# Fourth layer, first phase: two of four pairs of inner tiles by seven products of halves

## The chip, the cores and the metric

The kernel runs on one core of a Trainium2 chip. The metric is device time in microseconds (us) of one execution, as the median of several runs. Engines are called by short names: PE is TensorE, PEld its weight loads, DVE VectorE, ACT ScalarE, POOL GpSimd, and SP is the engine whose queue issues the loads and stores.

## The reference

Attention over 2 x 12 heads with scores capped by a tanh, then two feed-forward blocks on the 896 tokens that come out (2 batches of 448, 768 columns):

```python
scores = cap * np.tanh(scale * q @ k.T / cap)
x = softmax(scores) @ v                    # as (896, 768)
h = x @ w_in;   x = maximum(h, 0) ** 2 @ w_out       # w_in 768 x 2048, w_out 2048 x 768
h = x @ w2_in;  return h / (1 + exp(-h)) @ w2_out    # same shapes
```

## The kernel before, in words

**Layers and tiles.** After the attention there are four layers: a (times `w_in`, relu squared), b (`w_out`), c (`w2_in`, silu) and d (`w2_out`). The inner dimension of 2048 is cut into 16 inner tiles of 128, the tokens into two halves b of S = 448, the 768 outputs into six blocks of 128 rows m (two halves n of three). Every f32 operand is held as two f16 parts, high and low, and a product of blocks is three matmuls of 128x128 by 128x448 (`products`, L902): high by high, and each high by the other's low. The rounding part `high` is made by `act` (L844) or `dve` (L858), the rest by `low_part` (L202).

**Phases.** The layers alternate: a0 b0 a1 b1 a2 b2 c0 d0 c1 d1. Each phase of a or c makes a group of inner tiles, the phase of b or d behind it uses them at once. The plan "f" (L175) has phases of 4, 6 and 6 inner tiles in a and b, and 8 and 8 in c and d.

**Pairs.** `Pair` (L914) makes two inner tiles by two halves of tokens from halves of operands: seven products of halves, p1 to p7, each nine matmuls, in the place of eight. Three accumulator banks are reused, so ACT copies a bank away (k1 behind p1, k2 behind p6) before the product that overwrites it. For layer d as a consumer, the same scheme needs forms of the activations (`forms_of_blocks`, L1086: four subtractions and four splits for each pair) and of the weights (`pair_steps`, L392: four sums of halves and splits of 768, 768, 768 and 384 columns, in place of two of 768).

**Layer d.** Its first phase (d0) goes through `out_units` (L1124): 12 outputs (six row blocks by two halves), each 4 pairs of inner tiles deep, 24 matmuls in a bank. `end2` (L1235) copies a bank to a tile y2 with ACT, and SP sends it to DRAM, tensor `spill` (L1248). The second phase (d1, L1256 to L1350) does its four pairs by seven, in two groups of two pairs (`GROUP`); it brings y back from `spill` with 12 loads on SP into the tile that held the forms of x1 (L1257 to L1259), so they wait for the last product of c1, and DVE adds a bank to y in `sum_of` (L1262):

```python
            y3 = x1.rows()
            for n, b in ((1, 1), (0, 1), (0, 0), (1, 0)):
                for m in range(MN * n, MN * n + MN):
                    nc.sync.dma_start(half(y3[:, m], b), spill[m, :, b * S : b * S + S])
```

**What sets the order of the rest.** Weights arrive bent as integers, and are turned (ACT `head` L340, DVE `shift` L348), split into high and low f16 parts (L364) and kept in slots: 14 tiles of 768 columns (`hl`), taken as a ring (`slot` L286), and small ones for the rests. `Plan` (L121) says when each is used; `Stream.chunk` (L505) lays background steps of ACT and DVE between products by planned costs and due times. A step with an alternative (`either`, L193) changes engine if its own is further behind than `SLACK` (0.3). Tiles of intermediate results are a ring of seven (`rtile`, L881). `Forms` (L1352) does the same as a pair's forms for the input of c, called x1.

Of the kernel before, what the change touches and what calls it, by code (L numbers as in the profile page):

```python
# [26 lines left out]
def softcap_attention_relu2_silu(  # L27
# [90 lines left out]
    GROUP = 2  # L118
    PLAIN = (("a", 0), ("a", 2))

    class Plan:  # L121
# [3 lines left out]
        def __init__(self, *sizes, seven=()):  # L125
            self.seven = seven
            self.items, self.where, self.layer, self.use, self.starts = [], {}, [], {}, []
            self.t, self.most, self.phases = 0.0, max(sum(sizes, ())), {}
# [4 lines left out]
            self.paired = {self.where[w, f] for w in "ac" for f in range(0, FT, 2) if (w, f) not in PLAIN}  # L133
            self.paired |= {self.where[w, 0, f // KD] for w, ph in seven for f in range(*self.phases[w][ph], KD)}

        def add(self, w_i, w_o, a, b):
            t, use, where, items = self.t, self.use, self.where, self.items
            self.starts.append(t)
            for f0, f1 in self.phases[a]:
# [13 lines left out]
                if (b, self.phases[a].index((f0, f1))) in self.seven:  # L153
                    stage = KT // 2 * GROUP * UNIT / 4
                    for e in range(e0, e1):
                        for n in range(DM // NW):
                            i = where[b, n, e] = len(items)
                            items.append((tile_of(w_o, n * (FT // KD) + e), f"w{b}{n}_{e}"))
                            self.layer.append(b)
                        at = t + (e - e0) % GROUP * UNIT / 4  # L160
                        use[i - 1], use[i - 1, "s"] = at, at + 2 * stage
                        use[i], use[i - 1, "r"] = at + 4 * stage, at + 5 * stage
                        if (e - e0) % GROUP == GROUP - 1:
                            t += 7 * stage
# [95 lines left out]
    class Stream:  # L260


        def __init__(self, plan, tag, wpool, dt, watch):
# [1322 lines left out]
```

## Time and profile before

| what | us |
|---|---|
| median of 3 runs (503.84 to 504.8) | 503.94 |
| the profiled execution | 504.16 |
| its span in the trace | 502.3 |
| busy: PE, DVE, ACT | 492.3, 392.1, 340.9 |
| stage starts: a0, b0, a1, b1 | 87.1, 114.3, 141.6, 177.3 |
| a2, b2, c0 | 218.2, 254.3, 295.2 |
| d0, c1, d1, last PE work | 343.9, 398.4, 446.1, 496.4 |

The profiled execution's own time is 1.86 us longer than the span of its instructions. The stage starts are the first matmul of each stage on PE's timeline. The names of tiles in the rows carry the stage: `ac8f` is a bank of layer c at inner tile 8, `yd_0f` an output bank of d0, `p_4df` a bank of d1's first group (pairs 4 and 5), `yformsf` the forms of activations, `yf` the tile of y.

### The profile page before, as it was taken

How to read it: one execution, taken by the hardware profiler on the slowest of the kernel's cores; microseconds unless marked ns; L12 is line 12 of the kernel's file. 1: busy time of each engine (PE TensorE's matmuls, PEld its weight loads, DVE VectorE, ACT ScalarE, POOL GpSimd, SP SyncE). 2: the span in 40 equal slices, each digit the busy share in tenths (PEclk: the TensorE clock that was granted, in tenths of full speed). 3: DMA queues.
4: the chain of work that ended last, by engine and by line, in shares of the span. 5: the costliest groups of instructions: out<-in, count | busy, mean ns of one | idle time of the engine just before them, and what ended most of it. 6: DMA issues, size and time to landing. Idle time of an engine off the chain costs nothing.

```text
span 502.3 us, 7110 instructions
## 1 busy us (share of the span) xinstructions
PE 492.3 (98%) x2608; PEld 237.9 (47%) x2608; DVE 392.1 (78%) x770; ACT 340.9 (68%) x524; POOL 31.6 (6%) x33
## 2 busy tenths in 40 slices
PE   8999999999999999999999999999999999998995
PEld 4233233555555555554555554555555555554552
DVE  0778999999978898967888988889143469987863
ACT  5999995978779984568985668987242487670200
POOL 1002555300000000000000000000000000000000
PEclk9999999999999999999999999999999999999999
DMA  7746562234544554773341215643517122033014
GB/s 253 264 140 168 175 190 66 90 112 162 178 147 165 190 189 133 244 253 125 125 128 62 64 63 190 217 161 130 191 42 243 61 88 98 0 103 117 2 74 153
DMA packets 22387, 69.76 MB, mean 139 GB/s; under 512 B 2887, under 2 KB 14151, under 8 KB 22343
## 3 DMA queue, kind: packets, MB, share of 16 engines
q1 hardware_dynamic: 22308, 69.22, 41.5%
q8 instruction: 22, 0.36, 0.3%
q14 instruction: 23, 0.18, 0.1%
q0 software_dynamic: 32, 0.00, 0.0%
q10 hardware_dynamic: 2, 0.00, 0.0%
HBM read 63.64 MB, written 5.54 MB: 138 GB/s over the span
## 4 chain that ended last, share of the span: by engine, by line
PE 93%; ACT 2%; DMA 1%; DVE 1%; issue 1%; SPq 0%; DVEq 0%
PE px L633 7%; PE p_6df L906 4%; PE yb_5f L906 4%; PE yb_3f L906 4%; PE yb_1f L906 4%; PE yb_0f L906 4%; PE yb_4f L906 4%; PE yb_2f L906 4%; PE s_B L614 3%; PE s_A L614 3%; PE ha_0f L906 3%; PE ha_1f L906 3%; PE p_4df L906 2%; PE yd_3f L906 2%; PE yd_5f L906 2%; PE yd_4f L906 2%
## 5 line engine op out<-in xcount | busy, mean ns | idle before, releaser
L622 ACT ACTIVATE e_A<-s_A 128x896 f32<-128x896 f32 x18 | 15.9, 918 | 4.5 <-PE s_A L614 4.2
L622 ACT ACTIVATE e_B<-s_B 128x896 f32<-128x896 f32 x18 | 15.9, 917 | 3.9 <-PE s_B L614 3.6
L718 ACT ACTIVATE e_A<-e_A 128x896 f32<-128x896 f32 x18 | 16.5, 955 | 0.0
L718 ACT ACTIVATE e_B<-e_B 128x896 f32<-128x896 f32 x18 | 16.5, 953 | 0.0
L1265 DVE SCALAR_TENSOR_TENSOR yf<-p_6df,yf 128x448 f32<-128x448 f32 x15 | 9.2, 623 | 6.1 <-PE p_6df L906 6.1
L207 DVE SCALAR_TENSOR_TENSOR hl_64f<-u_64f,hl_64f 128x768 f16<-128x768 f32 x1 | 1.0, 957 | 15.9 <-ACT hl_64f L373 15.9
L653 DVE TENSOR_TENSOR total<-total,e_C 64x896 f32<-64x896 f32 x11 | 12.9, 1172 | 0.4
L207 DVE SCALAR_TENSOR_TENSOR hl_68f<-u_69f,hl_68f 128x768 f16<-128x768 f32 x1 | 1.0, 959 | 13.1 <-ACT hl_68f L373 13.1
L1265 DVE SCALAR_TENSOR_TENSOR yf<-p_4df,yf 128x448 f32<-128x448 f32 x15 | 9.0, 614 | 0.0
L207 DVE SCALAR_TENSOR_TENSOR x1f<-yaf,x1f 128x448 f16<-128x448 f32 x12 | 7.3, 619 | 1.7 <-ACT x1f L845 1.7
L649 DVE TENSOR_TENSOR total<-total,e_A 128x896 f32<-128x896 f32 x6 | 8.2, 1359 | 0.3
L845 ACT ACTIVATE x1f<-yaf 128x448 f16<-128x448 f32 x12 | 6.7, 571 | 2.3 <-DVE yaf L856 2.2
L647 DVE TENSOR_TENSOR total<-e_A,e_A 128x896 f32<-128x896 f32 x6 | 6.6, 1102 | 1.2 <-ACT e_A L718 1.2
L373 ACT ACTIVATE hl_80f<-u_81f 128x768 f16<-128x768 f32 x1 | 0.8, 843 | 9.9 <-DVE u_81f L398 9.9
L856 DVE TENSOR_TENSOR yaf<-yaf 128x448 f32<-128x448 f32 x12 | 7.4, 620 | 0.1
L845 ACT ACTIVATE ycf<-yd_4f 128x448 f32<-128x448 f32 x2 | 1.1, 544 | 8.0 <-PE yd_4f L906 8.0
L647 DVE TENSOR_TENSOR total<-e_B,e_B 128x896 f32<-128x896 f32 x5 | 6.5, 1294 | 0.0
L706 DVE RECIPROCAL r<-r 128x448 f32<-128x448 f32 x2 | 5.9, 2954 | 0.1
L236 ACT ACTIVATE junk<-x0f 128x896 bf16<-128x896 f16 x6 | 5.7, 947 | 0.3
L906 PE MATMUL p_4df<-yformsf,hl_72f 128*128 128x448 f16 x18 | 4.4, 352 | 1.5 <-DVE yf L1265 1.5
L649 DVE TENSOR_TENSOR total<-total,e_B 128x896 f32<-128x896 f32 x5 | 5.5, 1091 | 0.4
L731 DVE TENSOR_SCALAR gcap<-gcap 128x1 f32<-128x1 f32 x1 | 0.2, 155 | 7.2 <-ACT gcap L730 7.2
(1848 smaller groups left out, 1646.0 us busy)
## 6 DMA issues: line engine op xcount, KB each, us to landing
spill<-ycf SPq DMA_DIRECT2D x12, 224.0 KB, 1.9
yf<-spill SPq DMA_DIRECT2D x12, 224.0 KB, 5.3
out<-yf SPq DMA_DIRECT2D x12, 224.0 KB, 2.2
rb<-scratch SPq DMA_DIRECT2D x10, 224.0 KB, 3.9
raw_wb_0f<-in_moe_w_out SPq DMA_DIRECT2D x2, 768.0 KB, 5.7
raw_wb_1f<-in_moe_w_out SPq DMA_DIRECT2D x2, 768.0 KB, 4.3
raw_wb_2f<-in_moe_w_out SPq DMA_DIRECT2D x2, 768.0 KB, 4.3
raw_wb_3f<-in_moe_w_out SPq DMA_DIRECT2D x2, 768.0 KB, 4.3
```

Of the source, the lines that this page charges most:

```text
L207: nc.vector.scalar_tensor_tensor(lo, x, scale, hi, op0=ALU.mult, op1=ALU.subtract, accum_out=watch.low() if see else None)
L614: nc.tensor.matmul(sp[:, j, :S] if b is None else sp[head(b), j, :S], lhsT=qk[head(j), 1, 128 * c : min(128 * c + 128, S)], rhs=qk[head(j) ...
L622: nc.scalar.activation(t, sp[:, :, :S], AF.Tanh, scale=scale_s)
L633: nc.tensor.matmul(px[i][head(j), :S], lhsT=v_m[:, 3 * j + int(x[1])] if b is None else pr.vc[m][head(b), j], rhs=e[:, j] if b is None els ...
L647: nc.vector.tensor_tensor(t, ex[m, x[0] + "0"], e, op=ALU.add)
L649: nc.vector.tensor_tensor(total[i], total[i], e, op=ALU.add)
L653: nc.vector.tensor_tensor(t, t, ex[m, "C"][head(b)], op=ALU.add)
L718: nc.scalar.activation(ex[m, x], ex[m, x], AF.Exp, scale=scale_c)
L845: return Step("A", cols, lambda: nc.scalar.activation(at(out), at(src), func, scale=scale), list(deps))
L856: return Step(eng, cols, lambda: e.tensor_tensor(at(out), at(x), at(y), op=op), list(deps))
L906: nc.tensor.matmul(acc, lhsT=w(e_w, kk), rhs=x(e_x, kk), start=first and i == 0, stop=last and i == len(n) - 1, skip_group_check=more,)
L1265: return Step("D", S, lambda: nc.vector.scalar_tensor_tensor(yb, acc, to_y, yb, op0=ALU.mult, op1=ALU.add), list(deps))
```

## The change

In d0, pairs 0 and 1 (the first four inner tiles) go by seven products, and pairs 2 and 3 are accumulated plainly into the same banks: p2, p3 and p4 each carry a plain part for one of the outputs (0,0), (0,1) and (1,0), and a new bank "z" takes (1,1). `Plan` takes a table of groups for each phase. The results of d0 are now kept in tiles of the ring `rtile`, the first contribution by an ACT copy, later ones by DVE sums, and are spilled from there. `forms_tile` runs whatever steps of x1's forms are left before the forms of c's pairs are laid where they are. Slots for weights go to the one that is planned free first. `SLACK` is 1.0 for 0.3, `CAUTION` 0.5 for 0.6. Samples for the self-test of numbers are taken at other tiles.

```diff
--- before.py
+++ after.py
...
@@ -172,13 +176,13 @@
                     t += (e1 - e0) * KT // 2 * UNIT
             self.t = t

-    plans = {"f": Plan((4, 6, 6), (8, 8), seven=(("d", 1),)), "g": Plan((4, 4, 4, 4), (4, 4, 4, 4))}
+    plans = {"f": Plan((4, 6, 6), (8, 8), seven={("d", 0): (((0, 1),), (2, 3)), ("d", 1): (((0, 1), (2, 3)), ())}), "g": Plan((4, 4, 4, 4), (4, 4, 4, 4))}

     ACT_FIX, ACT_COL = 0.11, 0.00082
     DVE_FIX, DVE_COL = 0.075, 0.00105
     POOL_FIX, POOL_COL = 0.1, 0.0036
     HOP = 0.21
-    SLACK, CAUTION = 0.3, 0.6
+    SLACK, CAUTION = 1.0, 0.5
     LOAD, NEXT_LOAD = 4.5, 3.1

     class Step:
...
@@ -285,17 +289,17 @@

         def slot(self, i):
             if i not in self.hl:
-                j = len(self.slots)
-                self.slots.append(i)
-                at = j % self.nslots
+                j = len(self.hl)
+                at = self.freest(self.slots, self.nslots)[1]
+                self.slots[at] = i
...

         def rest(self, i):
             if i not in self.hl:
-                at = len(self.rests) % self.nrests
-                self.rests.append(i)
+                at = self.freest(self.rests, self.nrests)[1]
+                self.rests[at] = i
...
@@ -306,14 +310,18 @@
                 self.u[i] = self.wpool.tile([128, WT], F32, tag="u", bufs=self.nwords, name=f"u_{len(self.u)}{self.tag}")
             return self.u[i]

+        def freest(self, held, n):
+
+            return min((-1.0 if at not in held else self.freed.get(held[at], 1e9), at) for at in range(n))
+
         def is_free(self, key):
             if key[1:] == ("r",) if isinstance(key, tuple) else False:
-                n = len(self.rests)
-                return -1.0 if n < self.nrests else self.freed.get(self.rests[n - self.nrests])
-            n = len(self.slots)
-            if next(k for k in self.order if k not in self.hl) != key:
+                t = self.freest(self.rests, self.nrests)[0]
+            elif next(k for k in self.order if k not in self.hl) != key:
                 return None
-            return -1.0 if n < self.nslots else self.freed.get(self.slots[n - self.nslots])
+            else:
+                t = self.freest(self.slots, self.nslots)[0]
+            return t if t < 1e9 else None

         def room(self):
...
@@ -921,7 +929,7 @@
                 self.i = i = ws.todo.where[w, f]
                 self.forms = self.forms_at(i)
                 self.open, self.seeded = False, True
-                self.four = watch and (NEXT[w], [f0 <= f < f1 for f0, f1 in phases[w]].index(True)) in ws.todo.seven
+                self.four = ws.todo.where.get((NEXT[w], 0, f // KD)) in ws.todo.paired
                 self.blocks = {}

             @staticmethod
...
@@ -1113,6 +1122,18 @@
                 split("p7", r12, [t3], 9.0)
                 split("p4", r21, [t4], 10.0)
                 ends[ended[id(r11)]] = t2
+
+        forms_of = {}
+
+        def forms_tile():
+            if f0 not in forms_of:
+                for st in x1.steps:
+                    if st.end is None:
+                        ws.run_first(st)
+                forms_of[f0] = ytile("forms").rearrange("p m s -> p (m s)").bitcast(F16).rearrange(
+                    "p (n e s) -> p n e s", e=2, s=S
+                )
+            return forms_of[f0]

         def run_pairs(w, fs, x, funcs):
             for f in fs[::2]:
...
@@ -1221,15 +1242,12 @@
         for ph in range(len(phases["c"])):
             f0, f1 = phases["c"][ph]
             fs = range(f0, f1)
-            seven = ("d", ph) in ws.todo.seven
+            seven, plain = ws.todo.seven.get(("d", ph), ((), ()))
+            final = ph == len(phases["c"]) - 1
...
-            if seven:
-                forms = ytile("forms").rearrange("p m s -> p (m s)").bitcast(F16).rearrange(
-                    "p (n e s) -> p n e s", e=2, s=S
-                )
             run_pairs("c", fs, x1, silu)
-            if ph == 0:
+            if ph == 0 and not seven:
                 y2 = ytile("c")

...
@@ -1253,18 +1269,27 @@
...

-            y3 = x1.rows()
-            for n, b in ((1, 1), (0, 1), (0, 0), (1, 0)):
-                for m in range(MN * n, MN * n + MN):
-                    nc.sync.dma_start(half(y3[:, m], b), spill[m, :, b * S : b * S + S])
-            accs, steps = {}, {}
+            if final:
+                y3 = x1.rows()
+                for n, b in ((1, 1), (0, 1), (0, 0), (1, 0)):
+                    for m in range(MN * n, MN * n + MN):
+                        nc.sync.dma_start(half(y3[:, m], b), spill[m, :, b * S : b * S + S])
+            accs, steps, rows = {}, {}, {}

             def sum_of(n, b, m, acc, deps=()):

-                yb = half(y3[:, MN * n + m], b)
-                return Step("D", S, lambda: nc.vector.scalar_tensor_tensor(
-                    yb, acc, to_y, yb, op0=ALU.mult, op1=ALU.add
-                ), list(deps))
+                if final or (n, b, m) in rows:
+                    yb = rows[n, b, m] if not final else half(y3[:, MN * n + m], b)
+                    st = Step("D", S, lambda: nc.vector.scalar_tensor_tensor(
+                        yb, acc, to_y, yb, op0=ALU.mult, op1=ALU.add
+                    ), list(deps))
+                else:
+                    yb, free = rtile(f"y{n}{b}{m}")
+                    rows[n, b, m] = yb
+                    st = act(AF.Copy, yb, acc, free, scale=to_y)
+                if not final:
+                    ends[ended[id(yb)]] = st
+                return st

             def new(name, pool):
                 if pool == "q":
@@ -1274,15 +1299,18 @@
             def operand(p, f, e):
                 if p in ("p1", "p2", "p5", "p3"):
                     return half(g[f + (p in ("p2", "p3"))][:, e], int(p in ("p5", "p3")))
-                return forms[:, 3 * ((f - f0) // 2) + ("p6", "p7", "p4").index(p), e]
+                return forms_tile()[:, 3 * ((f - f0) // 2) + ("p6", "p7", "p4").index(p), e]

             def stored(n, b, m):
+                if not final:
+                    nc.sync.dma_start(spill[MN * n + m, :, b * S : b * S + S], rows[n, b, m])
+                    return
                 m += MN * n
                 if es[-1] < f1 // KD - 1:
                     return
                 nc.sync.dma_start(out[m * 128 : m * 128 + 128, b * S : b * S + S], half(y3[:, m], b))

-            def ended(p, m):
+            def behind(p, m):

                 us = UNIT / 4
                 if p == "p1":
@@ -1301,22 +1329,51 @@
...
                     st = steps["k3", m] = sum_of(1, 1, m, accs["a", m], [steps["k5", m]])
                     ws.chunk(us, st)
-                    stored(1, 1, m)
+                    if not plain:
+                        stored(1, 1, m)
                 elif p == "p3":
                     ws.chunk(us, sum_of(0, 1, m, accs["b", m], [steps["k2", m]]))
                     stored(0, 1, m)
-                else:
+                elif p == "p4":
                     ws.chunk(us, sum_of(1, 0, m, accs["a", m]))
                     stored(1, 0, m)
+                else:
+                    ws.chunk(us, sum_of(1, 1, m, accs["z", m], [steps["k3", m]]))
+                    stored(1, 1, m)

             needs = {"p2": "k1", "p6": "k1", "p7": "k2", "p3": "k5", "p4": "k3"}
...
-            groups = [range(e, e + GROUP) for e in range(f0 // KD, f1 // KD, GROUP)]
-            for es, p in [(es, p) for es in groups for p in ("p1", "p2", "p5", "p6", "p7", "p3", "p4")]:
-                for m, e in [(m, e) for m in range(MN) for e in es]:
+            def plain_products(p, m, e):
+
+                (n, b), bk = {"p2": ((0, 0), "c"), "p3": ((0, 1), "b"), "p4": ((1, 0), "a"), "z": ((1, 1), "z")}[p]
+                if (bk, m) not in accs:
+                    accs[bk, m] = new(f"z{m}", "p")
+                key = ws.todo.where["d", n, e]
+                hl = ws.get(key)
+                for kk in range(KD):
+                    ws.need(done[KD * e + kk, b])
+                first, last = p == "z" and e == f0 // KD + plain[0], e == f0 // KD + plain[-1]
+                products(
+                    accs[bk, m], lambda ew, kk: hl[:, ew, kk * NW + m * 128 : kk * NW + m * 128 + 128],
+                    lambda ex, kk: half(g[KD * e + kk][:, ex], b), range(KD), first, last, p != "z",
+                )
+                if m == MN - 1 and p in ("p3", "z"):
+                    ws.used(key)
+                if last:
+                    ws.chunk(UNIT / 4)
+                    behind(p, m)
+                else:
+                    ws.chunk(UNIT / 2)
+
+            order = ("p1", "p2", "p5", "p6", "p7", "p3", "z", "p4") if plain else ("p1", "p2", "p5", "p6", "p7", "p3", "p4")
+            groups = [range(f0 // KD + es[0], f0 // KD + es[-1] + 1) for es in seven]
+            for es, p in [(es, p) for es in groups for p in order]:
+                for m, e in [(m, e) for m in range(MN) for e in es] if p != "z" else ():
                     f, i = KD * e, ws.todo.where["d", 0, e]
                     key, at = Pair.forms_at(i)[p]
                     hl = ws.get(key)
+                    if watch and (ph, p, m, e) == (0, "p1", 0, 0):
+                        watch_later(hl[:, 0, :S])
                     if p in of_block:
                         k, b = of_block[p]
                         ws.need(done[f + k, b])
@@ -1330,22 +1387,26 @@
                     fresh = p in ("p1", "p5")
                     products(
                         acc, lambda ew, kk: hl[:, ew, at + m * 128 : at + m * 128 + 128],
-                        lambda ex, kk: operand(p, f, ex), range(1), fresh and e == es[0], e == es[-1], not fresh,
+                        lambda ex, kk: operand(p, f, ex), range(1), fresh and e == es[0],
+                        e == es[-1] and not (plain and p in ("p2", "p3", "p4")), not fresh,
                     )
                     if m == MN - 1 and p in ("p2", "p6", "p3", "p4"):
                         ws.used(key)
-                    if e == es[-1]:
-                        ended(p, m)
+                    if e == es[-1] and not (plain and p in ("p2", "p3", "p4")):
+                        behind(p, m)
                     else:
                         ws.chunk(UNIT / 4)
...
+                if p in ("p2", "p3", "p4", "z"):
+                    for e, m in [(f0 // KD + e, m) for e in plain for m in range(MN)]:
+                        plain_products(p, m, e)
...
```

On each engine the order moves as follows. On PE, the program has 18 matmuls and 18 weight loads fewer, all of them in d0 (270 for 288). The first place is DVE at the start of d1, from the first sum with the reloaded y on (`c_4df` and `p_4df` are banks, `hl` and `hr` weights, `gc` activations, `u` turned weights). Before:

```order
L1265 SCALAR_TENSOR_TENSOR yf<-c_4df,yf 128x448
L207 SCALAR_TENSOR_TENSOR gc14f,lows<-c11c14f,gc14f 128x448
L1265 SCALAR_TENSOR_TENSOR yf<-c_4df,yf 128x448
L856 TENSOR_TENSOR s5c14f<-s5c14f,c11c14f 128x448
L1265 SCALAR_TENSOR_TENSOR yf<-c_4df,yf 128x448
L856 TENSOR_TENSOR c21c14f<-c21c14f,s5c14f 128x448
L1265 SCALAR_TENSOR_TENSOR yf<-p_4df,yf 128x448
L207 SCALAR_TENSOR_TENSOR hl_77f,lows<-u_78f,hl_77f 128x768
L1265 SCALAR_TENSOR_TENSOR yf<-p_4df,yf 128x448 x2
L207 SCALAR_TENSOR_TENSOR yformsf,lows<-s5c14f,yformsf 128x448
L1265 SCALAR_TENSOR_TENSOR yf<-p_4df,yf 128x448
```

and in the change:

```order
L211 SCALAR_TENSOR_TENSOR gc14f,lows<-c11c14f,gc14f 128x448
L1283 SCALAR_TENSOR_TENSOR yf<-c_4df,yf 128x448
L864 TENSOR_TENSOR s5c14f<-s5c14f,c11c14f 128x448
L1283 SCALAR_TENSOR_TENSOR yf<-c_4df,yf 128x448
L864 TENSOR_TENSOR c21c14f<-c21c14f,s5c14f 128x448
L1283 SCALAR_TENSOR_TENSOR yf<-c_4df,yf 128x448
L211 SCALAR_TENSOR_TENSOR yformsf,lows<-u2c14f,yformsf 128x448
L1283 SCALAR_TENSOR_TENSOR yf<-p_4df,yf 128x448
L211 SCALAR_TENSOR_TENSOR yformsf,lows<-s5c14f,yformsf 128x448
L1283 SCALAR_TENSOR_TENSOR yf<-p_4df,yf 128x448 x2
L211 SCALAR_TENSOR_TENSOR yformsf,lows<-c21c14f,yformsf 128x448
L1283 SCALAR_TENSOR_TENSOR yf<-p_4df,yf 128x448
```

Both pieces end with the same sum, the seventh. The low part of the wide weight `hl_77f` and that of `gc14f` no longer stand among the sums; two more low parts of `yformsf` do.

The second place is SP's queue during d0 and c1, which issues the loads of weights (`raw_w...`) and the spills. Before:

```order
L281 DMA raw_wc15f<-in_moe_w_in 128x6144
L281 DMA raw_wd_4f<-in_moe_w_out 128x6144 x2
L1248 DMA spill<-ycf 128x448 x7
L281 DMA raw_wd_5f<-in_moe_w_out 128x6144 x2
L1248 DMA spill<-ycf 128x448
L281 DMA raw_wd_6f<-in_moe_w_out 128x6144
L1248 DMA spill<-ycf 128x448 x4
```

and in the change:

```order
L1306 DMA spill<-y002f 128x448
L285 DMA raw_wd_4f<-in_moe_w_out 128x6144 x2
L285 DMA raw_wd_5f<-in_moe_w_out 128x6144
L1306 DMA spill<-y010f 128x448
L1306 DMA spill<-y011f 128x448
L1306 DMA spill<-y012f 128x448
L285 DMA raw_wd_5f<-in_moe_w_out 128x6144
L1306 DMA spill<-y110f 128x448
L1306 DMA spill<-y111f 128x448
```

The spills stand singly or in threes between the loads, each from a tile of its own.

The third place is ACT in a0 (`x0` is the input, `ha` banks and tiles of layer a, `ga` its outputs, `zeros` the head of a turned weight). Before:

```order
L373 ACTIVATE hl_3f<-u_3f 128x768
L236 ACTIVATE junk,squares<-x0f 128x896 x6
L845 ACTIVATE ha_0f<-ha_0f 128x448 x3
L845 ACTIVATE ga0f<-ha_0f 128x448
L845 ACTIVATE ha_1f<-ha_1f 128x448 x3
L845 ACTIVATE ga0f<-ha_1f 128x448
L845 ACTIVATE ha_1f<-ha_1f 128x448
L845 ACTIVATE ga1f<-ha_1f 128x448
```

and in the change:

```order
L381 ACTIVATE hl_3f<-u_3f 128x768
L240 ACTIVATE junk,squares<-x0f 128x896 x4
L853 ACTIVATE x0f<-x_c11f 128x448
L853 ACTIVATE x_f0f<-x_c0f 128x448
L240 ACTIVATE junk,squares<-x0f 128x896
L354 ACTIVATE zeros<-raw_wb_1f 128x768
L853 ACTIVATE ha_0f<-ha_0f 128x448 x3
L853 ACTIVATE ga0f<-ha_0f 128x448
L853 ACTIVATE ha_1f<-ha_1f 128x448
```

The two forms of x0 were DVE's work before, and the weight `raw_wb_1f` is turned earlier.

## Rows read from the trace of the kernel before

**Rows 1.** Page: span, and per engine busy us (share of the span) xinstructions.

```profile
span 502.3 us, 7110 instructions
...
PE 492.3 (98%) x2608; PEld 237.9 (47%) x2608; DVE 392.1 (78%) x770; ACT 340.9 (68%) x524; POOL 31.6 (6%) x33
```

**Rows 2.** Page, the chain that ended last, shares of the span by engine.

```profile
PE 93%; ACT 2%; DMA 1%; DVE 1%; issue 1%; SPq 0%; DVEq 0%
```

**Rows 3.** Busy time by stage: a0, c0, d0, c1 and d1 in that order.

```profile
core 0: us, PE busy (x) PEld busy (x) DVE busy (x) ACT busy (x) POOL busy (x), PEclk, DMA share, GB/s
87.10:114.30 27.20, 27.20 (x146) 14.08 (x145) 26.60 (x51) 22.26 (x39) 4.41 (x5) 1.00 0.33 113
...
295.20:343.90 48.70, 48.02 (x253) 24.63 (x252) 41.87 (x94) 42.10 (x71) 0.00 (x0) 1.00 0.51 172
343.90:398.40 54.50, 54.50 (x290) 28.18 (x288) 20.70 (x47) 20.10 (x30) 0.00 (x0) 1.00 0.35 125
398.40:446.10 47.70, 47.70 (x255) 24.66 (x252) 42.02 (x103) 36.17 (x61) 0.00 (x0) 1.00 0.17 55
446.10:496.40 50.30, 48.48 (x255) 24.66 (x253) 37.26 (x85) 9.11 (x16) 0.00 (x0) 1.00 0.29 100
```

**Rows 4.** Timeline (start us, us, engine): first matmul of d0, of c1.

```profile
343.95 0.35 PE L906 MATMUL yd_0f<-gc0f,hl_50f 128*128 128x448 f16 x1
...
398.43 0.92 PE L906 MATMUL ac8f<-x1f,hl_58f 128*128 128x448 f16 x4
```

**Rows 5.** Page, groups: line engine op out<-in xcount | busy, mean ns | idle.

```profile
L207 DVE SCALAR_TENSOR_TENSOR hl_64f<-u_64f,hl_64f 128x768 f16<-128x768 f32 x1 | 1.0, 957 | 15.9 <-ACT hl_64f L373 15.9
...
L207 DVE SCALAR_TENSOR_TENSOR x1f<-yaf,x1f 128x448 f16<-128x448 f32 x12 | 7.3, 619 | 1.7 <-ACT x1f L845 1.7
...
L845 ACT ACTIVATE x1f<-yaf 128x448 f16<-128x448 f32 x12 | 6.7, 571 | 2.3 <-DVE yaf L856 2.2
...
L1265 DVE SCALAR_TENSOR_TENSOR yf<-p_4df,yf 128x448 f32<-128x448 f32 x15 | 9.0, 614 | 0.0
...
L373 ACT ACTIVATE hl_80f<-u_81f 128x768 f16<-128x768 f32 x1 | 0.8, 843 | 9.9 <-DVE u_81f L398 9.9
...
L856 DVE TENSOR_TENSOR yaf<-yaf 128x448 f32<-128x448 f32 x12 | 7.4, 620 | 0.1
...
L845 ACT ACTIVATE ycf<-yd_4f 128x448 f32<-128x448 f32 x2 | 1.1, 544 | 8.0 <-PE yd_4f L906 8.0
```

**Rows 6.** Timeline of DVE at the start of d1.

```profile
449.51 0.38 DVE L850 TENSOR_SCALAR yformsf<-u2c14f 128x448 f16<-128x448 f32 x1
...
454.94 0.62 DVE L1265 SCALAR_TENSOR_TENSOR yf<-c_4df,yf 128x448 f32<-128x448 f32 x1 [4.38 <-DMA yf<-spill]
```

**Rows 7.** Timeline of PE at its longest waits.

```profile
303.57 0.35 PE L906 MATMUL ac0f<-x_c0f,hl_40f 128*128 128x448 f16 x1 [0.63 <-ACT u2c0f L845]
...
233.31 0.35 PE L906 MATMUL ba12f<-x_f4f,hl_27f 128*128 128x448 f16 x1
233.90 0.35 PE L906 MATMUL aa12f<-x_c3f,hl_27f 128*128 128x448 f16 x1 [0.24 <-ACT ca12f L845]
...
461.84 0.73 PE L906 MATMUL p_4df<-yformsf,hl_72f 128*128 128x448 f16 x3 [1.53 <-DVE yf L1265]
```

**Rows 8.** Waits of SP: waiting line <- releaser: us in all, times, longest.

```profile
SPq L1259 <- PE ac14f L906: 24.6, 1, 24.6
```

**Rows 9.** All waits of PE after the attention (87.1 us on).

```profile
PE p_4df L906 <- DVE yf L1265: 1.8, 2, 1.5
PE ac0f L906 <- ACT u2c0f L845: 0.6, 1, 0.6
PE aa12f L906 <- ACT ca12f L845: 0.2, 1, 0.2
```

**Rows 10.** Timeline of ACT, the copy that PE waits for at 233.90.

```profile
233.33 0.53 ACT L845 ACTIVATE ca12f<-aa12f 128x448 f32<-128x448 f32 x1
```

More of the change, by code (lines that the diff above doesn't have):

```diff
@@ L117, in softcap_attention_relu2_silu, with __init__ @@
     PROD, UNIT = 9 * COL2, 12 * COL2
-    GROUP = 2
     PLAIN = (("a", 0), ("a", 2))
     class Plan:
-        def __init__(self, *sizes, seven=()):
+        def __init__(self, *sizes, seven={}):
             self.seven = seven
             self.items, self.where, self.layer, self.use, self.starts = [], {}, [], {}, []
-            self.t, self.most, self.phases = 0.0, max(sum(sizes, ())), {}
+            self.t, self.most, self.phases, self.paired = 0.0, max(sum(sizes, ())), {}, set()
             for w_i, w_o, a, b, size in ((w_in, w_out, "a", "b", sizes[0]), (w2_in, w2_out, "c", "d", sizes[1])):
@@ L132, in __init__ @@
                 self.add(w_i, w_o, a, b)
-            self.paired = {self.where[w, f] for w in "ac" for f in range(0, FT, 2) if (w, f) not in PLAIN}
-            self.paired |= {self.where[w, 0, f // KD] for w, ph in seven for f in range(*self.phases[w][ph], KD)}
+            self.paired |= {self.where[w, f] for w in "ac" for f in range(0, FT, 2) if (w, f) not in PLAIN}
         def add(self, w_i, w_o, a, b):
@@ L152, in add @@
                 e0, e1 = f0 // KD, f1 // KD
-                if (b, self.phases[a].index((f0, f1))) in self.seven:
-                    stage = KT // 2 * GROUP * UNIT / 4
+                groups, plain = self.seven.get((b, self.phases[a].index((f0, f1))), ((), ()))
+                if groups:
                     for e in range(e0, e1):
                         for n in range(DM // NW):
-                            i = where[b, n, e] = len(items)
+                            where[b, n, e] = len(items)
                             items.append((tile_of(w_o, n * (FT // KD) + e), f"w{b}{n}_{e}"))
                             self.layer.append(b)
[L160 to L164, printed above, removed]
+                    for es in groups:
+                        stage, more = KT // 2 * len(es) * UNIT / 4, KT // 2 * len(plain) * UNIT / 2
+                        for k, e in enumerate(es):
+                            i, at = where[b, 0, e0 + e], t + k * UNIT / 4
+                            self.paired.add(i)
+                            use[i], use[i, "s"] = at, at + 2 * stage + more
+                            use[i + 1], use[i, "r"] = at + 4 * stage + more, at + 5 * stage + more
+                        for e in plain:
+                            use[where[b, 0, e0 + e]] = t + 2 * stage
+                            use[where[b, 1, e0 + e]] = t + 6 * stage + 2 * more
+                        t += 7 * stage + 4 * more
                     continue
@@ L269, in __init__ @@
             self.raw, self.hl, self.ready, self.freed = [], {}, {}, {}
-            self.turned, self.slots, self.rests, self.order, self.u = [], [], [], [], {}
+            self.turned, self.slots, self.rests, self.order, self.u = [], {}, {}, [], {}
             self.words, self.read = [], {}
@@ L991, in out @@
                 a, self.done[ff, bb] = parts(r, hi, lo, after, to_g[self.w], self.w == "c")
-                if watch and ff == 0:
+                if watch and self.f == 0 and (ff, bb) in ((0, 0), (1, 1) if self.four else (0, 1)):
                     watch_later(hi, a)
@@ L1246, in end2 @@
                 ws.chunk(us, st)
-                if ph == 0 and ws.todo.seven:
-                    nc.sync.dma_start(spill[m, :, b * S : b * S + S], yb)
                 if ph == len(phases["c"]) - 1:
@@ L1378, in __init__, with later @@
             self.dt, self.scale, self.seen = dt, scale, {}
-            self.cells, self.more = {}, {}
+            self.cells, self.more, self.steps = {}, {}, []
             self.ready, self.highs, self.given, self.plain_end = {}, {}, set(), None
+        def later(self, *steps):
+            self.steps += steps
+            self.ws.later(*steps)
         def rows(self):
@@ L1418, in look @@
             c.due = self.due["p4", 0] - 4.0 if key in (1, 2) else self.ws.now + 60.0
-            self.ws.later(c)
+            self.later(c)
         def late(self, *last):
@@ L1432, in late @@
                         s.due = self.due[self.OWN[i % 4], i // 4] - 2.0
-                    self.ws.later(*own)
+                    self.later(*own)
                     st = own[-1]
@@ L1450, in split @@
             self.ready[p, j] = b
-            self.ws.later(a, b)
+            self.later(a, b)
             return b
@@ L1465, in minus @@
                 t.due = self.due[p, j] - 2.0
-                self.ws.later(t)
+                self.later(t)
                 return t
```

7 lines of the change are left out of this document (4 added, 3 removed).

## The prediction

> **What bounds the kernel now.** I read the page's busy shares first: TensorE (PE) is busy for 492.3 of a span of 502.3 us, VectorE (DVE) for 392.1 and ScalarE (ACT) for 340.9 [rows 1]. The chain of work that ended last says the same of the end: 93% of it is PE [rows 2]. An average hides stages, so I cut the span at the first matmul of each stage [rows 3]. In a0, c0, d0 and c1 PE is busy for the whole stretch or all but 0.7 us. Only d1 loses more: 48.48 busy of 50.30. So a change is worth the PE time that it removes, less what the other engines then add as waits, and the second is judged from DVE and ACT in the same rows. They are near full in c0 (41.87 and 42.10 of 48.70) and half idle in d0 (20.70 and 20.10 of 54.50).
>
> All PE work has one price. Layer d's first phase runs from 343.95 to 398.43 without a gap [rows 4]: 54.48 us for 12 outputs of 24 matmuls, 288 in all, or 0.1892 us for each, start to start.
>
> **The change, part by part.**
>
> *Products.* Plain, two inner tiles against two halves of the columns and two halves of the tokens are eight block products; the pairs cost seven. Per phase d0: the seven take 7 x 3 blocks of rows x 2 pairs x 3 split products = 126 matmuls, the two plain pairs 4 x 3 x 2 x 2 x 3 = 144, together 270 for 288. No other stage's count changes. That is 18 x 0.1892 = **-3.40 us**. All of it lies on the path, as rows 4 has no gap in which it could hide.
>
> *Work added for the seven forms*, by engine. Forms of the activations: 2 pairs x 4 subtractions x 0.620 = 5.0 on DVE; seven low parts in place of four for each pair, so 6 x 0.619 = 3.7 on DVE and 6 high parts x 0.571 = 3.4 on ACT. Forms of the weights: per pair four half-width sums (0.62 is their upper bound, from a wider tile) and 1.5 more splits, at most two at 0.957 on DVE and two at 0.843 on ACT: at most 2 x (2.5 + 1.9) = 8.8 and 2 x 1.7 = 3.4. Ends: 9 sums on DVE, which read a bank as the low parts read a tile, x 0.619 = 5.6, and 15 copies on ACT for 12, + 3 x 0.544 = 1.6 [rows 5]. DVE gets about 23 us, ACT 8.4. The order puts most of this into d0, whose DVE had 34 us idle; c0, c1 and d0 keep each engine below PE when I add up their instructions by these durations (c0: DVE some 3 us more, 45 of 48). The two pairs done by seven are those whose activations come out of the first half of c0, and their p6 and p7 come 17 and 20 us into d0 (p1, p2 with its plain part and p5 stand ahead: 18 + 54 + 18 matmuls). I cost the added work at **nothing**; its cover is PE's unbroken row of products, and if that cover fails the price is rival B's.
>
> *Moves between DVE and ACT.* The new slack makes the planner leave work on ACT that it used to hand over: 27 high parts go from a DVE form of 0.38 us to an ACT form of 0.571 [rows 5, 6]. DVE is relieved of 10 us, ACT takes 15. In a0 ACT was busy for 22.26 of 27.20 [rows 3]; about 4 us more still fit. The Trainium skill, page "ScalarE: Activation LUTs", section "Rules for kernel authors", speaks against this move: multiplications are better on VectorE than on ScalarE. The trace agrees on the single instruction, 0.38 against 0.571. Obeyed, it says that 27 x 0.19 = 5.1 us of engine time are wasted; whether that is time of the kernel depends on ACT setting an end, which is rival C. My sum counts zero.
>
> *The start of d1.* PE waits 1.53 us for a sum of DVE, at 461.84 [rows 7]. DVE itself had waited 4.38 us for the reload of y from the spill [rows 6], which SP issues only when PE's last product of c1 is done [rows 8]. The reload, its queue position and its trigger do not change, so the DVE wait stays. From the first sum to the seventh, which PE wants, DVE does 7 sums, 2 subtractions and 3 low parts, before as after; but before one of the three was the wide one of a weight (0.957 for 0.619), and it now lies ahead of the DVE wait. That saves about 0.33; a weight's shift now stands between two later sums and may give back some 0.15. I take **-0.2**; the ends are 0 and -0.33.
>
> *Spills and queues.* The 12 spills of d0 now leave from short-lived tiles and stand among the weight loads on SP, five loads behind a spill that waits for a sum. A late sum delays a load, thence weights. By the order those five bring weights of d1 and of c's last pair, used a stage later; and all that PE waits for after the attention is two sums of DVE and two copies of ACT, no load and no weight [rows 9], so nothing is charged. Slots in any order remove some DVE and ACT waits for a slot; PE has none of these, nothing again.
>
> Sum: -3.40 - 0.2 = -3.6. The profiled execution took 504.16 us, 0.22 more than the median of 503.94. So 504.16 - 3.60 = 500.56 there, and **500.3 us** for the median. Its own range is 499.7 to 501.2: DVE's stall of d1 wholly unmoved, or one or two new ACT waits of 0.4 as in rows 7, above; a little more recovered, below.
>
> **The rivals.**
>
> *A. The small stalls go as well.* Freer DVE and slots could remove the 0.40 that PE loses between 233.31 and 233.90 (0.59 for a step of 0.19) behind an ACT copy and the larger part of d1's wait (1.53). Against: the copy stood in an ACT queue without a gap ahead of it [rows 7, 10], and ACT gets more work. For: slots no longer taken in a ring, so that conversions spread out. 500.3 - 0.4 - 0.5 = 499.4 us.
>
> *B. DVE comes late in c0.* DVE goes from 42 to 45 of 48.7 there, and the first forms now force all leftover form steps of x1 out at once. Then each of c0's four pairs loses between 0.2 and the 0.8 that PE loses at 303.57 today (a start-to-start step of 0.98 for 0.189) [rows 7]: 0.8 to 3.1, so 501.1 to 503.4, in the middle 502.3 us. For it: the narrowest DVE margin of the program. Against: the added forms are due only in d0, with 17 us in hand.
>
> *C. ACT becomes the bound; slower.* Every pair of layers a and c has two products (p6, p7) that wait for an ACT copy of a bank (k1, k2). One other product of nine matmuls, 1.70 us, lies between; the copy takes 0.544, so ACT may be 1.1 us late before PE feels it. The wait of 0.24 before 233.90 is this case already [rows 7, 10]. With ACT at some 365 us for 341, and long forms of 0.84 in front of the copies, being late at each costs 14 pairs x 2 x 0.2 = 5.6 us, more than the products give: 500.3 + 5.6 = 505.9 us. It decides from an ACT backlog of more than 1.1 us at most copies. Against: of 28 copies two are felt now, and ACT has 18% free or more outside c0, where it gains nothing. The rule of the Trainium skill above would come out here: its 5.1 us, if all of them lay on the path, give 505.4.
>
> That the change doesn't do what it says is no rival: the order of PE has the 18 matmuls fewer.
>
> **How the numbers follow.** Chances: forecast 0.63, A 0.13, B 0.17, C 0.07. The range of 8 in 10 reaches from A's end to the lower half of B: **499.2 to 502.4**; outside lie C, the dearer part of B and some surprise below. Two tenths of a per cent, 1.0 us, is about what a measurement can tell from no change: faster means below 502.9, slower above 505.0. Faster: forecast, A and most of B, 0.87; same: B's dear end and a weak C, 0.08; slower: the rest of C, 0.05.
>
> **What would show it.** Right: d0 at about 51.1 us (270 x 0.1892) with no gap; c0 and c1 within 0.3 us of 48.6 and 47.7; d1's stall on the sum between 1.2 and 1.6; DVE busy in d0 above 30. B shows as PE waits for DVE in c0 and a c0 over 49.5; C as PE waits for ACT copies, many of them, in a1, a2 and c; A as a d1 below 49.8. The prediction is wrong if d0 keeps 54 us or if one stage other than d0 changes by more than 0.7 us.

## The result

The changed kernel takes 507.82 us (median of 7 runs, 505.8 to 510.91); the kernel before took 503.84 beside it. The ratio is 1.0077, 95% interval 1.005 to 1.0104: slower by 0.8%, where 0.7% faster was forecast. The profiled execution took 507.26.

The page of the changed kernel, span and busy time by engine, which answer to [rows 1]:

```profile
span 505.5 us, 7155 instructions
...
PE 490.9 (97%) x2590; PEld 236.5 (47%) x2590; DVE 397.3 (79%) x769; ACT 367.0 (73%) x589; POOL 30.8 (6%) x33
```

PE has less to do, as forecast, and the span is 3.2 us longer all the same. The stretches c0, d0, c1 and d1 in the view by stage (columns as in [rows 3]: length, then busy us of PE, PEld, DVE, ACT, POOL, granted clock, DMA share, GB/s):

```profile
294.30:343.70 49.40, 48.03 (x255) 24.66 (x253) 43.06 (x105) 40.85 (x75) 0.00 (x0) 1.00 0.29 97
343.70:394.75 51.05, 51.05 (x271) 26.40 (x270) 34.09 (x68) 26.67 (x42) 0.00 (x0) 1.00 0.49 170
394.75:450.55 55.80, 50.40 (x254) 25.30 (x253) 44.22 (x108) 40.44 (x70) 0.00 (x0) 0.94 0.23 78
450.55:499.65 49.10, 48.45 (x255) 24.65 (x253) 34.55 (x78) 9.39 (x17) 0.00 (x0) 1.00 0.29 102
```

From first matmul to first matmul, before and after: c0 48.76 and 49.35, **d0 54.48 and 51.08**, **c1 47.67 and 55.78**, d1 50.28 and 49.08. The attention and the six stages of a and b together are 0.9 shorter: a2 took 35.75 for 36.15, and the wait for `ca12f` of [rows 9] is gone, while a0 began 0.47 earlier, which lies within the 0.7 by which that start differs between the profiled executions here. So d0 gave its 3.40 us to the hundredth, d1 gave 1.2, and c1, whose products the change does not touch, took 8.1. Next, all that PE waits for in the changed kernel, which answers to [rows 9]:

```profile
PE bc8f L914 <- ACT y100f L853: 3.6, 1, 3.6
PE ac8f L914 <- ACT cc8f L853: 1.8, 1, 1.8
PE ac0f L914 <- ACT u2c0f L853: 1.3, 1, 1.3
...
PE p_4df L914 <- DVE yf L1283: 0.6, 1, 0.6
```

The first two are new, stand at the start of c1, and are copies on ACT. The timeline of PE there:

```profile
394.76 1.87 PE L914 MATMUL ac8f<-x1f,hl_72f 128*128 128x448 f16 x9
400.21 0.35 PE L914 MATMUL bc8f<-x_f0f,hl_73f 128*128 128x448 f16 x1 [3.59 <-ACT y100f L853]
...
401.95 0.58 PE L914 MATMUL bc8f<-x_f4f,hl_73f 128*128 128x448 f16 x1
404.34 0.53 PE L914 MATMUL ac8f<-x_c3f,hl_73f 128*128 128x448 f16 x1 [1.81 <-ACT cc8f L853]
404.67 0.58 PE L914 MATMUL ac8f<-x_c7f,hl_73f 128*128 128x448 f16 x1
```

The first product of c1 runs, then PE stands 3.59 us, does nine matmuls, stands 1.81 more. From about 401.5 the steps are 0.37 instead of 0.19: the clock, in the same stretch by windows.

```profile
401.50:408.20 6.70, 4.89 (x15) 1.93 (x13) 1.04 (x3) 3.08 (x6) 0.00 (x0) 0.50 0.63 213
```

Granted 0.50 there, that is 1.2 GHz of 2.4. The clock had stayed at 1.00 through the first stop (396.5 to 400.2). Between the end of its first product, near 396.6, and 401.5 PE had done six or seven matmuls. Counted from the step lengths, the two waits cost 3.8 and 2.2 us and the half clock another 2.2.

ACT, whose copies PE wants, in the same stretch:

```profile
377.93 0.84 ACT L381 ACTIVATE hl_84f<-u_69f 128x768 f16<-128x768 f32 x1 [2.56 <-PE p_0df L914]
391.55 0.84 ACT L381 ACTIVATE hl_85f<-u_71f 128x768 f16<-128x768 f32 x1 [12.78 <-PE p_0df L914]
...
399.64 0.53 ACT L853 ACTIVATE y100f<-p_0df 128x448 f32<-128x448 f32 x1
401.97 1.06 ACT L354 ACTIVATE zeros<-raw_wd_6f 128x768 f16<-128x768 bf16 x1 [1.80 <-DMA raw_wd_6f<-in_moe_w_out]
402.90 0.52 ACT L853 ACTIVATE y101f<-p_0df 128x448 f32<-128x448 f32 x1
403.31 0.55 ACT L853 ACTIVATE y102f<-p_0df 128x448 f32<-128x448 f32 x1
403.73 0.56 ACT L853 ACTIVATE cc8f<-ac8f 128x448 f32<-128x448 f32 x1
```

Here is the cause in one row: ACT stands 12.78 us, from 378.77 to 391.55, at the high part of the weight `hl_85f`, waiting for a product of PE (`p_0df`, in that stretch p4 of d0). Behind it in ACT's queue are two more heads and four more splits, then the copy `y100f` that frees a bank for `bc8f`, a head that waits 1.80 for a load, and `cc8f` (k1) only after that.

What product is that? `hl_85f` is laid into the slot of `hl_69f`, the n=1 weight of the first plain pair. The view of the tile `hl_69f` names who waited for it, and PE's timeline shows its last reader, in p4, just ahead of the split's start at 391.55:

```profile
who waited for it (us, times):
  ACT hl_85f L381: 12.8, 1
```

```profile
391.16 0.35 PE L914 MATMUL p_0df<-gc5f,hl_69f 128*128 128x448 f16 x1
391.35 0.35 PE L914 MATMUL p_0df<-gc6f,hl_71f 128*128 128x448 f16 x1
```

In the changed code that slot is declared free here:

```diff
+                if m == MN - 1 and p in ("p3", "z"):
+                    ws.used(key)
```

The n=1 weights are read by z and by p4, and the order of d0 is p1, p2, p5, p6, p7, p3, z, p4: z is not the last reader. The semaphores still protect the data, so ACT waits for p4; but the planner, which lays ACT's queue and takes "the slot that is free first", has the slot free 10.2 us too early: PE turns to the next weight at 381.14 in z, and at 391.35 in p4.

### The profile page after: what moved, and what is told of

It is laid out like the page before. It is cut to its first block, busy times and chain, and to the rows that moved or that the text cites. A ratio compares the mean times of both kernels' runs of the same rounds, so it can differ in the third digit from the quotient of the medians.

```text
span 505.5 us, 7155 instructions
## 1 busy us (share of the span) xinstructions
PE 490.9 (97%) x2590; PEld 236.5 (47%) x2590; DVE 397.3 (79%) x769; ACT 367.0 (73%) x589; POOL 30.8 (6%) x33
## 4 chain that ended last, share of the span: by engine, by line
PE 93%; DMA 2%; ACT 2%; DVE 1%; issue 1%; SPq 0%; DVEq 0%; ACTq 0%
PE px L641 7%; PE p_0df L914 7%; PE p_6df L914 4%; PE yb_4f L914 4%; PE yb_0f L914 4%; PE yb_5f L914 4%; PE yb_3f L914 4%; PE yb_2f L914 4%; PE yb_1f L914 4%; PE s_B L622 3%; PE s_A L622 3%; PE ha_0f L914 3%; PE ha_1f L914 3%; PE p_4df L914 2%; PE c_0df L914 2%; PE ac8f L914 1%
## 5 line engine op out<-in xcount | busy, mean ns | idle before, releaser
L853 ACT ACTIVATE c_6df<-p_6df 128x448 f32<-128x448 f32 x3 | 1.6, 528 | 6.5 <-PE p_6df L914 6.5
L914 PEld LDWEIGHTS <-hl_73f 128*128 128x128 f16 x18 | 2.2, 125 | 8.6 <-issue 7.9
```

The source lines that it names most:

```text
L853: return Step("A", cols, lambda: nc.scalar.activation(at(out), at(src), func, scale=scale), list(deps))
L914: nc.tensor.matmul(acc, lhsT=w(e_w, kk), rhs=x(e_x, kk), start=first and i == 0, stop=last and i == len(n) - 1, skip_group_check=more,)
```

## The experiments

Three theories. **M**: the mark behind z. **L**: ACT has too much to do since SLACK is 1.0, and is late whatever the slots (the forecast's rival C). **E**: the ends of d0 fall on c1's first pair and wait for tiles that are still being spilled.

**The mark moved** (`mark_p4`).

```diff
-                if m == MN - 1 and p in ("p3", "z"):
+                if m == MN - 1 and p in ("p3", "p4"):
```

> The changed kernel, with the two weights of the plain tiles of outputs n=1 declared free behind p4 instead of behind z, the product that comes before p4. Theory M (mark): ACT stood 12.78 us at the split hl_85f because its slot was declared free behind z while p4 still read it; the late copies y100f and cc8f then stopped PE in c1. Expected 507.8 - 8.2 (c1 took 55.8 us for 47.6) = 499.6 us, c1 within 0.3 of 47.7, no halved clock. Theory L (load): ACT is late at the end of d0 because SLACK 1.0 leaves it too much work, wherever a slot is marked: stays at 505 to 508. Theory E (ends): the copies of d0's last three outputs fall on c1's first pair and wait for tiles whose spill is under way: stays above 503.

Measured: 499.64 us (499.25 to 499.99) against 503.3 of before, ratio 0.9929 (0.9912 to 0.9945). Windows of c1 and d1, and ACT's timeline at the end of d0:

```profile
395.04:442.70 47.66, 47.66 (x253) 24.66 (x252) 38.39 (x96) 36.09 (x64) 0.00 (x0) 1.00 0.18 63
442.70:492.20 49.50, 48.47 (x255) 24.66 (x253) 34.68 (x79) 9.39 (x17) 0.00 (x0) 1.00 0.29 100
```

```profile
387.86 0.84 ACT L381 ACTIVATE hl_86f<-u_71f 128x768 f16<-128x768 f32 x1 [4.61 <-PE p_0df L914]
...
391.83 0.84 ACT L381 ACTIVATE hl_88f<-u_72f 128x768 f16<-128x768 f32 x1 [1.43 <-PE p_0df L914]
392.97 0.54 ACT L853 ACTIVATE y100f<-p_0df 128x448 f32<-128x448 f32 x1 [0.29 <-PE p_0df L914]
...
396.94 0.53 ACT L853 ACTIVATE cc8f<-ac8f 128x448 f32<-128x448 f32 x1 [0.43 <-PE ac8f L914]
```

c1 is back at 47.66 with no wait and a full clock. The weight that was `hl_85f` is now `hl_86f` and takes a slot that the p4 of the pairs gives up; ACT waits 4.61 us for it, to 387.86, and the copy `cc8f` starts 1.9 us after c1's first matmul, where it had started 9.0 us after. Theory M holds. That its number is met to 0.04 us is in part chance: the kernel before was 0.54 faster in this round than beside the result, and against it the step is 7.6, not 8.2 us.

**The order turned instead** (`z_last`): the mark stays behind z, and z becomes the last product.

```diff
-            order = ("p1", "p2", "p5", "p6", "p7", "p3", "z", "p4") if plain else ("p1", "p2", "p5", "p6", "p7", "p3", "p4")
+            order = ("p1", "p2", "p5", "p6", "p7", "p3", "p4", "z") if plain else ("p1", "p2", "p5", "p6", "p7", "p3", "p4")
```

> The changed kernel with the mark as it was, but the order of d0 turned so that p4 comes before z: then z is the last reader and the mark is right. Theory M: about 499.6 us, as with the mark moved, c1 near 47.7. Theory L: 505 to 508, since ACT has the same work. Theory E: above 503, since three ends (then DVE sums) still fall on c1's start.

Measured: 500.24 us (499.7 to 500.35), ratio 0.9939 (0.9922 to 0.9955), with no wait of PE in c1. The mark line is untouched and the loss is gone, so it is the mark against the order of products that counts. E falls with `mark_p4`, which keeps the order of the ends: one copy does wait there for a tile that is being spilled (`s5c8f`, 1.18 us for the spill of `y101f`), and PE waits nowhere in c1. In `z_last` the last ends are DVE sums into tiles that are already there, so this run says little on E.

**Less for ACT** (`slack_old_mark`).

```diff
-    SLACK, CAUTION = 1.0, 0.5
+    SLACK, CAUTION = 0.3, 0.6
```

> The changed kernel with SLACK 0.3 and CAUTION 0.6 as before the change, mark untouched. Theory M: the split hl_85f still waits for the slot that p4 reads, ACT stands some 12 us, c1 stays at 53 to 56 us, in all 505 to 509. Theory L: ACT gets back its old share, no wait in c1, about 500.

Measured: 508.93 us (506.98 to 509.04), ratio 1.0102 (1.008 to 1.0125). The waits of PE, then of ACT:

```profile
PE bc8f L914 <- ACT y100f L853: 4.1, 1, 4.1
PE ac8f L914 <- ACT cc8f L853: 1.5, 1, 1.5
```

```profile
ACT hl_85f L381 <- PE p_0df L914: 11.6, 1, 11.6
```

The same split waits nearly as long, the same two products stop. L falls, as a cause of the loss in c1.

**Slots as a ring again** (`ring_old_mark`).

```diff
-                at = self.freest(self.slots, self.nslots)[1]
+                at = len(self.turns) % self.nslots
+                self.turns.append(i)
...
-                t = self.freest(self.slots, self.nslots)[0]
+                n = len(self.turns) - self.nslots
+                t = -1.0 if n < 0 else self.freed.get(self.turns[n], 1e9)
```

> The changed kernel with the wide slots taken as a ring again, mark untouched. By the order no split then falls on the slot of a plain weight while p4 reads it. Theory M: the 12.8 us wait is gone and c1's start with it, 499.5 to 502 (the ring delays other splits and may cost up to 2). Theory L and E: 505 to 508, as they do not depend on the slots.

Measured: 501.69 us (501.21 to 501.83), ratio 0.9969 (0.9956 to 0.9981). PE waits nowhere in c1, with the mark still wrong. One view corrects my reading of the cause:

```profile
ACT hl_80f L383 <- PE p_0df L916: 15.7, 1, 15.7
```

```profile
388.13 0.84 ACT L383 ACTIVATE hl_80f<-u_66f 128x768 f16<-128x768 f32 x1 [15.69 <-PE p_0df L916]
...
393.24 0.55 ACT L855 ACTIVATE y100f<-p_0df 128x448 f32<-128x448 f32 x1 [1.36 <-PE p_0df L916]
```

ACT stands even longer here at a slot, 15.7 us, and it costs PE nothing in c1. That the engine stands is thus not the price. Two things differ: the stop ends 7.2 us ahead of c1's first matmul (at 395.31), where it ended 3.2 us ahead in the changed kernel, and only four splits stand between it and `y100f`, where there were four splits and two heads, with two more waits of 1.2 us. The code offers a reason: this slot's weight is marked behind its true last reader, so the plan knew of the wait and laid the copies accordingly, and in the changed kernel it did not know. That reason is read from the code; no run separates the two differences. Of the 2.0 us above `mark_p4`, 1.7 lie in d1 (51.11 for 49.44), where PE waits 1.7 us for a sum and 0.6 for a weight.

**The rest of the change alone** (`d0_plain`): d0 plain, slots, SLACK and samples new.

```diff
-    plans = {"f": Plan((4, 6, 6), (8, 8), seven={("d", 0): (((0, 1),), (2, 3)), ("d", 1): (((0, 1), (2, 3)), ())}), "g": Plan((4, 4, 4, 4), (4, 4, 4, 4))}
+    plans = {"f": Plan((4, 6, 6), (8, 8), seven={("d", 1): (((0, 1), (2, 3)), ())}), "g": Plan((4, 4, 4, 4), (4, 4, 4, 4))}
...
                 ws.chunk(us, st)
+                if ph == 0 and ws.todo.seven:
+                    nc.sync.dma_start(spill[m, :, b * S : b * S + S], yb)
```

> The changed kernel with d0 plain again (288 matmuls, y2 copied and spilled as before), the rest of the change kept: slots in any order, SLACK 1.0, samples. Product theory: the other parts are worth nothing by themselves, so the time is that of mark_p4 (499.64) + 18 x 0.189 = 503.0, perhaps 0.7 less as the split hl_62f of a d0 weight no longer stands before the copies of c0's first pair: 502.3 to 503.1, no different from before (503.3). Rival: slots in any order and SLACK are what gained in mark_p4: 500 to 501.

Measured: 504.47 us (504.09 to 505.03) against 503.65, ratio 1.0014 (1.0005 to 1.0024). Not 502.3 to 503.1: without the seven products the other parts cost 0.7. PE's waits name where:

```profile
PE p_4df L914 <- DVE yf L1285: 1.2, 1, 1.2
...
PE ac2f L914 <- ACT cc2f L853: 1.0, 1, 1.0
PE ac0f L914 <- ACT u2c0f L853: 0.6, 1, 0.6
PE ac6f L914 <- ACT cc6f L853: 0.4, 1, 0.4
```

Two new waits for ACT copies in c0 (`cc2f`, `cc6f`, 1.4 together), a quarter of the 5.6 that rival C gave to late copies. Whether ACT's load makes them is not shown: it had itself stood at a weight's slot some 3 to 4 us ahead of each, 1.80 us at `hl_64f` and 1.24 at `hl_70f`.

```profile
307.92 0.84 ACT L381 ACTIVATE hl_64f<-u_54f 128x768 f16<-128x768 f32 x1 [1.80 <-PE ac0f L914]
...
311.71 0.52 ACT L853 ACTIVATE cc2f<-ac2f 128x448 f32<-128x448 f32 x1
```

The wait for `u2c0f` is 0.6, as before the change; in the kernels with seven products in d0 it is 1.3 (0.2 in `mark_p3_first` below, where c0's own order is turned). So that rise belongs to the seven products, and the timeline of ACT in `mark_p4` shows the instruction:

```profile
301.31 0.84 ACT L381 ACTIVATE hl_62f<-u_51f 128x768 f16<-128x768 f32 x1 [0.42 <-issue]
302.06 0.53 ACT L853 ACTIVATE c11c0f<-cc0f 128x448 f32<-128x448 f32 x1
...
303.10 0.53 ACT L853 ACTIVATE u2c0f<-ac0f 128x448 f32<-128x448 f32 x1
```

A split of a weight for d0 (0.84 us) stands directly ahead of the two copies; `u2c0f` begins 8.49 us into c0, where it began 7.79 in the kernel before, and c0 took 49.35 for 48.76. My cover of "nothing" for the added splits missed by these 0.6 to 0.7 us.

**A product between p6 and p7 of c0's first pair** (`mark_p3_first`).

```diff
-                    ("p3", range(1)), ("p6", late), ("p7", range(n)), ("p3", range(1, n)), ("p4", range(n)),
+                    ("p3", range(1)), ("p6", late), ("p3", range(1, n)), ("p7", range(n)), ("p4", range(n)),
```

> mark_p4 with the rest of p3 ahead of p7 in c0's first pair, so that two thirds of a product (6 x 0.189 = 1.13 us) lie between p6 and p7. The step of 1.67 before p7 (ACT copy u2c0f) should fall to 0.5 or less: 499.64 - 1.1 to 1.4 = 498.2 to 498.5. Rival: x1's forms for p3 are not ready then, and the wait only moves: 499.4 to 500.

Measured: 499.84 us (499.29 to 500.38), no gain over 499.64. PE's waits:

```profile
PE ac0f L914 <- DVE s5c0f L864: 0.7, 1, 0.7
...
PE ac0f L914 <- ACT u2c0f L853: 0.2, 1, 0.2
```

The wait for `u2c0f` fell from 1.3 to 0.2, and p4 now waits 0.7 for the sum behind p7, which nothing covers any more. c0 took 49.13 for 49.35. A miss: but for 0.2 us the wait moved by one product.

**The reload in another order** (`mark_reload`).

```diff
-                for n, b in ((1, 1), (0, 1), (0, 0), (1, 0)):
+                for n, b in ((0, 0), (1, 1), (0, 1), (1, 0)):
```

> mark_p4 with the reload of y ordered (0,0), (1,1), (0,1), (1,0). If DVE's wait of 3.11 us for the seventh piece is what makes PE wait in d1 (1.14 + 0.14 beyond the step), the sums start some 2.5 us earlier and PE's wait goes: 498.4, d1 at 48.2 for 49.5. Rival: DVE is as busy without it and the (1,1) pieces come late in turn: 499.4 to 499.7.

Measured: 498.69 us (498.57 to 498.72), ratio 0.9896 (0.9879 to 0.9913). PE no longer waits in d1, which took 48.16 for 49.44, and DVE's first sum waits for PE alone:

```profile
447.52 0.62 DVE L1283 SCALAR_TENSOR_TENSOR yf<-c_4df,yf 128x448 f32<-128x448 f32 x1 [0.24 <-PE c_4df L914]
```

In `mark_p4` DVE's wait for the seventh piece was thus what made PE wait. The kernel before shows the same chain [rows 6, 7], but this order was not tried on it.

**More pairs by seven** (`mark_three`, `mark_four`): in place of the groups (0, 1) plain (2, 3), groups (0, 1, 2) plain (3), and (0, 1, 2, 3) without a plain part.

> mark_p4 with three of d0's four pairs by seven and one plain: 7 x 3 x 3 x 3 + 4 x 3 x 2 x 3 = 189 + 72 = 261 matmuls for 270. Product theory, with the cover of DVE and ACT still whole: - 9 x 0.189 = -1.70, so 497.9. Rival: one pair's forms and weights more (by the sums of the prediction about 9 us of DVE, 4 of ACT) come late for d0 or c1, whose DVE is busy for 40 of 51 and 38 of 48 us: 499.5 or more, with PE waits for splits in d0 or c1.

> mark_p4 with all four pairs of d0 by seven in one group, no plain part and no bank z: 7 x 3 x 4 x 3 = 252 matmuls for 270. Product theory: 18 x 0.189 = 3.4 less than mark_p4's 499.64, so 496.2. mark_three gave 0.7 of its expected 1.7; if the cover goes on thinning, PE waits for forms or weights in d0 or c1: 497 to 500.

Measured: 498.95 us (498.56 to 499.27, ratio 0.9904, 0.9886 to 0.9921) and 524.56 us (523.17 to 525.91, ratio 1.042, 1.0394 to 1.0447). By the medians three pairs gave 0.7 of the 1.7 expected. In the profiled executions d0 is 49.37 for 51.08 and the span 496.3 for 498.0, 1.7 less each: the products gave what the sum says within d0. The medians show less for two reasons on record. The kernel before took 503.3 beside `mark_p4` and 503.65 beside `mark_three`, so against it the step is 1.04. And the time outside the span of instructions grew from 1.79 to 2.24 us by the medians of four executions (with the reload turned, below, it is 2.6); why is open. Four pairs lose 25 us, where 497 to 500 was expected at worst. The waits of PE with four:

```profile
PE p_0df L914 <- DVE hl_71f L211: 6.8, 1, 6.8
PE p_6df L914 <- DVE hl_103f L211: 6.0, 1, 6.0
PE p_4df L914 <- DVE hl_95f L211: 4.8, 1, 4.8
```

PE stands 6.8 us in d0 for the low part of `hl_71f`, a weight that the first two products want: p1 runs through the wide weights of four pairs, not two, at the very start of d0. From there the cover is gone, and d1 waits for its weights as well. Here, and not with two pairs, DVE comes late, though in d0 and d1 and not in c0, where rival B had put it: c0 took 49.36 us.

**Both** (`three_reload`, and the same with four pairs, `four_reload`).

> mark_three with the reload of y in the order of mark_reload. mark_three waits 1.0 us in d1 (0.8 for the sum of DVE); mark_reload took 0.95 from mark_p4. If both add up: 498.95 - 0.9 = 498.0. If DVE sets d1's start now and not the reload: 498.9.

> mark_four with the reload order of mark_reload: mark_four less 0.9 if d1 waits there for the reload as in mark_p4, 495.3 by the product theory; the same as mark_four if not.

Measured: 497.63 us (497.58 to 497.83), ratio 0.9887 (0.987 to 0.9903), the best of this study, 6 us under the kernel before; and 522.86 us (522.46 to 525.11), ratio 1.0399 (1.0371 to 1.0427). The gain of the reload adds up with three pairs; with four it took off 1.7 us, as the wait for the copy `c_4df` at d1's start fell from 3.2 to 1.9.

## Why the prediction was wrong

- *Products*, -3.40: right. d0 went from 54.48 to 51.08.
- *Start of d1*, -0.2: the sign right, the size short. In `mark_p4` d1 is 49.44 for 50.28, -0.8. DVE's wait for the reload, which I had held fixed, shrank from 4.38 to 3.11: the piece landed 7.6 us into d1 where it had landed 8.8 us into it. SP started its 12 loads within 5.6 us there and within 6.8 us in the kernel before, one issue of which took 1.2 us where the median is 0.43; the loads also landed faster, 4.5 us for 5.3 by the median. What slowed that one issue was not tried.
- *Work added, cover whole*: nearly right, 0.6 to 0.7 off, at `u2c0f`, as shown above. The move of work to ACT cost nothing that shows in `mark_p4`, where PE waits for ACT only at `u2c0f`. The Trainium skill (page "ScalarE: Activation LUTs", section "Rules for kernel authors") speaks against such a move, as it puts multiplications on VectorE. The prediction worked out 5.1 us for this from rows; no run shows such a loss, and what there is to measure points the other way. `slack_old_mark`, where the work goes back to DVE, differs from the changed kernel in `SLACK` and `CAUTION` alone, and up to the end of c0, ahead of the stop, their stages agree within 0.05 us, but for a2: 35.75 us with the work on ACT, 35.98 with it on DVE.
- *Slots*: here it failed. "Slots in any order remove some DVE and ACT waits for a slot; PE has none of these, nothing again." I asked what the old ring's waits were worth and not whether the new choice rests on times that are true. A free mark that stands before the last reader is harmless in a ring that comes round later, and harmful where the planner seeks out the earliest mark. The prediction put this term at nothing; the price was 507.82 - 499.64 = 8.2 us, or 7.6 us with each set against the kernel before beside it, more than twice the gain.
- *Rivals*: A's two gains came, though the forecast had put the first at nothing: the wait behind `ca12f` is gone and a2 is 0.40 shorter, in the changed kernel and in `mark_p4`, and d1 is below A's 49.8 in both, there by a reload that landed earlier and not by a freer DVE. C's number (505.9) lies near the result, but by a cause that did not occur: ACT was not overloaded, it stood 12.78 us. B did not occur with two pairs. None of the three had a queue stopped at one instruction. With the mark right, the forecast of 500.3 would have been 0.7 too high as a time; as a gain it was met, 3.6 forecast and 3.66 measured (503.3 to 499.64). That is in part luck: in the profiled executions a2 gave 0.40, d0 3.40 and d1 0.84, and c0 took 0.59.

## What to carry to other kernels

When a planner chooses by "free from", follow each mark to the last reader in the order of the program, above all where products have been put into a new order. An in-order queue that stops at an early instruction delays all behind it, and what it costs is read from what is queued behind and how soon that is needed, not from how long it stands (12.78 us cost c1 8.1 us, 15.7 us cost it nothing). A stop of PE may cost more than itself, as the clock can fall behind it.

## What had not been expected of the hardware

PE ran at 1.2 GHz for some 6.7 us (granted clock 0.50 from 401.5 to 408.2); before and in that stretch stand two waits of 3.59 and 1.81 us with nine matmuls between them. The slow clock made 2.2 of the 8.1 us. In `mark_four` a single stop of 6.80 us is followed by the same: granted 0.50 from 353.0 to 358.9, where sixteen matmuls took 2.9 us longer than at full clock. The single waits of the kernel before, the longest 1.53 us, left the clock at 1.00 in every stage of [rows 3]. The Trainium skill, page "TensorE: Matmul & The Clock Gate", section "HAM oscillation — how this bites in real kernels", says that pauses for data bring the slower clock back, which costs on top of the pause; the trace agrees, with these 2.2 us. The times of the changed kernel also spread more (505.8 to 510.91) than those of `mark_p4` (499.25 to 499.99); why is open. The mean granted clocks on record do not go with the times (0.996 at 507.82, 0.995 at 505.8, 0.992 at 510.91), and only one execution was profiled.
